# Local attention on block-diagonal keys and values, two heads at a time, in a fused attention and feed-forward kernel

## The chip, the cores and the metric

The kernel runs on one core of a Trainium2 chip. Times are device microseconds (us) of one execution. A run is called slow when it lies over 1.5% above the fastest of the same kernel; slow runs are left out of every ratio. The core has five engines that matter here: TensorE (PE in the profile; PEld is its weight load), VectorE (DVE), ScalarE (ACT), GpSimd (POOL) and SyncE (SP, which here only issues transfers). PEclk is the TensorE clock that was granted, as a share of full speed.

## The reference

```python
def _attn_ref(q, k, v):                      # each 8 batches x 8 heads x 576 x 64
    q_d, k_d, v_d = means of four rows       # 144 x 64
    out_d = sm_attn(q_d, k_d, v_d)           # full attention on the means
    out_up = np.repeat(out_d, 4, axis=2)
    mask = np.abs(pos[:, None] - pos[None, :]) < 4
    scores = np.where(mask, scale * q @ k.T, -1e9)
    out_local = softmax(scores) @ v          # a band of 7 keys
    return out_up + out_local

x = attention output, 4608 tokens x 512
out = gelu(x @ w_in) @ w_out                 # 512 -> 2048 -> 512, exact Gelu
```

So each batch has a small dense attention on 144 means, a banded one on 576 rows, and their sum feeds a feed-forward layer that carries most of the matrix work.

## The kernel before

The tokens are cut into nine chunks of 512. While TensorE does chunk c, the attention of batch c + 1 is woven into the gaps: its transposes into the first product (`m1`), its scores and values into the second (`m2`). `f1` and `f2` are fills: each call issues so many matmuls of the product.

```python
for c in range(NCH):
    b = c + 1
    f1 = filler(m1(c)) if c else f1_0
    ...
    elif b < B:
        v_down(b)                      # sums of four rows of v, five GpSimd instructions
        for p in range(NP):            # four pairs of heads
            f1(6 if p == 0 else 7)
            t_in(b, p, "q")
            f1(7)
            t_in(b, p, "k")
        k_lo()
    f1()
    f2 = filler(m2(c))
    ...
            attn(b, f2, 6, 9, 9)
    f2()
```

The local scores are five windows of 128 keys for each head, against a copy of k that is zero in the other head's rows. The values come out with the query on the partitions and a 65th column that sums the exponentials. VectorE divides by it, TensorE transposes the result back, and VectorE adds the two attentions into `xT`, the operand of the next first product.

```python
def norm(p, ps, half=None):
    ...
        nc.vector.reciprocal(out=rr, in_=av4[:, :, :, 64])
        nc.vector.tensor_tensor(out=nall..., in0=av4[:, :, :, 0:64], in1=rr..., op=ALU.mult)

def t_out(b, p):
    tr = ppool.tile([128, 1024], F16, tag="tr", name="tr_o")          # in PSUM
    ...                                                               # seven transposes
    nc.scalar.copy(out=xd, in_=tr[:, 576:720])
    nc.vector.tensor_tensor(out=xT[:, p, ...], in0=tr[:, 0:S]...,     # one operand in PSUM,
                            in1=xd.unsqueeze(2).broadcast_to(...), op=ALU.add)   # one in SBUF
```

The values of the next batch are loaded by GpSimd after each chunk. The output copies out of PSUM are on ScalarE. TensorE's two product banks alternate.

The softmax here doesn't subtract the row's maximum and nothing guards it: scores larger than these inputs give would overflow.

## Time and profile before

| | before |
|---|---|
| median of 3 runs | 353.62 us (352.41 to 353.96) |
| profiled span, granted clock | 348.4 us, 1.000 |
| TensorE busy | 97% |
| VectorE, ScalarE, GpSimd busy | 53, 55, 52% |
| one batch in the steady part | 20.33 + 15.89 = 36.22 us |

The prediction shows the lines behind this table. Two more stretches matter for what follows. The VectorE timeline of the first batch (start, us, engine, line, operation, output and input, count):

```profile
15.65 0.41 DVE L539 COPY q_nat<-q_nat 72x1024 f16<-72x1024 f16 x1
...
16.65 0.54 DVE L305 COPY KL<-kdz 64x64 f16<-64x64 f16 x2
```

These two copies go from SBUF to SBUF, and TensorE needs their results soon. They are short. The second stretch is a chunk boundary, from the timelines of GpSimd and VectorE:

```profile
143.29 1.27 POOL L312 TENSOR_TENSOR v_d<-v_t 128x512 f16<-128x512 f32 x1
...
144.17 0.76 DVE L445 TENSOR_TENSOR xT<-tr_o,xd 128x576 f16<-128x576 f16 x1 [2.11 <-ACT xd L444]
```

The add into `xT` takes 0.76 us while GpSimd is at its sums of v. Remember that its first operand, `tr_o`, lies in PSUM.

### The profile page before, as it was taken

What the parts mean: (1) busy time and instruction counts of PE and PEld (TensorE: products, weight loads), DVE (VectorE), ACT (ScalarE), POOL (GpSimd) and SP (SyncE); (2) the same over time, 40 slices, a digit from 0 to 9 for tenths busy, and PEclk for the clock granted to TensorE, in tenths of its full rate; (3) what the DMA queues carried; (4) which work ended last, traced back from release to release, by engine and by line L of the source; (5) the groups of instructions that cost most, each with busy time, mean ns of one, the idle gap of its engine ahead of it and who ended that gap; (6) DMA issues with size and microseconds to landing.
All of it is one profiled execution on the core that took longest, in us unless ns stands there. A gap on an engine that the chain in (4) does not pass through costs nothing.

```text
span 348.4 us, 7162 instructions
## 1 busy us (share of the span) xinstructions
PE 339.0 (97%) x2976; PEld 193.9 (56%) x2976; DVE 184.5 (53%) x338; ACT 192.8 (55%) x360; POOL 180.4 (52%) x243
## 2 busy tenths in 40 slices
PE   8898998999999999999999999999999999999996
PEld 4773455655665566555655575556655664444444
DVE  7793645747574857386747665676558470000000
ACT  3664465645764577357746764566556755614620
POOL 8957649633977298628963797369652000000000
PEclk9999999999999999999999999999999999999999
DMA  6999999920999099908990599129940001011002
GB/s 87 165 205 144 185 164 110 182 75 0 98 159 146 2 77 152 176 0 59 154 171 23 36 148 178 41 18 150 159 79 0 32 33 59 2 60 60 0 34 89
DMA packets 126543, 32.31 MB, mean 93 GB/s; under 512 B 109616, under 2 KB 122032, under 8 KB 126512
## 3 DMA queue, kind: packets, MB, share of 16 engines
q0 software_dynamic: 121184, 22.43, 82.2%
q1 hardware_dynamic: 5328, 9.44, 7.6%
q8 instruction: 23, 0.38, 0.4%
q14 instruction: 8, 0.07, 0.1%
HBM read 44.83 MB, written 9.44 MB: 156 GB/s over the span
## 4 chain that ended last, share of the span: by engine, by line
PE 88%; DMA 6%; DVE 2%; POOL 2%; issue 1%; ACT 0%; POOLq 0%
PE m_ps L224 35%; PE m_ps L200 33%; PE sc L348 4%; DMA w_in_sb<-in_moe_w_in_dram 3%; PE av L403 2%; PE tr_o L441 2%; DMA q_nat<-in_q_dram 2%; PE tr_k L237 2%; PE tr_q L237 2%; DMA k_nat<-in_k_dram 1%; DVE kz L272 1%; PE av L397 1%; PE sc L353 1%; PE m_ps L215 1%; PE av L395 1%; DVE kdz L275 1%
## 5 line engine op out<-in xcount | busy, mean ns | idle before, releaser
L200 PE MATMUL m_ps<-xT,w_in_sb 128*128 128x512 f16 x568 | 133.3, 379 | 0.5 <-ACT gT L195 0.5
L224 PE MATMUL m_ps<-w_out_sb,gT 128*128 128x512 f16 x560 | 130.3, 379 | 0.0
L203 ACT ACTIVATE gT<-m_ps 128x512 f16<-128x512 f32 x142 | 84.8, 597 | 56.7 <-PE m_ps L200 56.7
L200 PEld LDWEIGHTS <-w_in_sb 128*128 128x128 f16 x568 | 52.1, 97 | 54.7 <-issue 0.8
L224 PEld LDWEIGHTS <-gT 128*128 128x128 f16 x560 | 51.9, 98 | 54.6
L228 ACT COPY out_sb<-m_ps 128x512 f32<-128x512 f32 x35 | 20.6, 589 | 42.8 <-PE m_ps L224 37.8
L243 POOL TENSOR_TENSOR q_t<-qT 128x288 f32<-128x288 f16 x24 | 16.0, 667 | 52.0 <-DVE qT L240 37.8
L104 POOL DMA_DIRECT2D q_nat<-in_q_dram x42 | 32.6, 789 | 8.1 <-DMA w_out_sb<-in_moe_w_out_dram 5.7
L252 DVE TENSOR_REDUCE kdz<-kz 64x144 f16<-64x576 f16 x48 | 35.9, 747 | 1.5
L445 DVE TENSOR_TENSOR xT<-tr_o,xd 128x576 f16<-128x576 f16 x28 | 21.2, 758 | 26.9 <-ACT xd L444 26.9
L104 POOL DMA_DIRECT2D k_nat<-in_k_dram x42 | 32.2, 778 | 6.3 <-DMA w_in_sb<-in_moe_w_in_dram 3.5
L418 DVE TENSOR_TENSOR nall<-av,rr 128x896 f16<-128x896 f32 x29 | 31.7, 1091 | 1.0
L248 DVE COPY kz<-tr_k 64x576 f16<-64x576 f16 x48 | 21.9, 455 | 18.2 <-PE tr_k L237 17.5
L381 DVE TENSOR_TENSOR e<-e,band 128x1152 f16<-128x1152 f16 x28 | 21.0, 751 | 17.6 <-ACT e L375 17.6
L219 DVE COPY out_sa<-m_ps 128x256 f32<-128x256 f32 x2 | 0.8, 424 | 54.9 <-PE m_ps L215 54.9
L116 POOL DMA_DIRECT2D v_win<-in_v_dram x30 | 26.6, 912 | 0.0
L348 PE MATMUL sc<-qT,kz 128*128 128x112 f16 (+1 forms) x320 | 25.6, 214 | 0.0
L373 ACT ACTIVATE e<-sc 128x680 f16<-128x680 f32 x32 | 23.4, 732 | 2.0 <-PE sc L348 2.0
L348 PEld LDWEIGHTS <-kz 128*128 128x128 f16 x320 | 21.6, 97 | 0.9
L311 POOL TENSOR_TENSOR v_t<-v_grp 128x1024 f32<-128x1024 f16 x6 | 12.7, 2118 | 17.0 <-DMA v_grp<-in_v_dram 17.0
L444 ACT COPY xd<-tr_o 128x144 f16<-128x144 f16 x28 | 7.7, 276 | 22.0 <-PE tr_o L441 22.0
L375 ACT ACTIVATE e<-sc 128x472 f16<-128x472 f32 x32 | 18.2, 569 | 0.0
(168 smaller groups left out, 407.6 us busy)
## 6 DMA issues: line engine op xcount, KB each, us to landing
out_dram<-out_sb SPq DMA_DIRECT2D x35, 256.0 KB, 3.2
v_win<-in_v_dram POOLq DMA_DIRECT2D x40, 128.0 KB, 9.6
q_nat<-in_q_dram POOLq DMA_DIRECT2D x42, 96.0 KB, 3.7
k_nat<-in_k_dram POOLq DMA_DIRECT2D x42, 96.0 KB, 4.2
v_grp<-in_v_dram POOLq DMA_DIRECT2D x6, 512.0 KB, 8.8
w_in_sb<-in_moe_w_in_dram POOLq DMA_DIRECT2D x4, 512.0 KB, 8.1
w_out_sb<-in_moe_w_out_dram POOLq DMA_DIRECT2D x4, 512.0 KB, 9.4
v_lo<-in_v_dram POOLq DMA_DIRECT2D x6, 64.0 KB, 8.8
```

Of the source, the lines that this page charges most:

```text
L104: nc.gpsimd.dma_start(out=nat6(ld[b % 2][nm])[:, c, :, :], in_=src[b, :, CH * c:CH * c + CH, :].rearrange("h s d -> s h d"))
L116: nc.gpsimd.dma_start(out=L["vw"][:, j, :, 0:64], in_=v[b, :, W0[j]:W0[j] + 128, :].rearrange("h s d -> s h d"))
L200: nc.tensor.matmul(out=ps, lhsT=w_in_sb[:, fc, 128 * j:128 * j + 128], rhs=xT[:, fc, 512 * c:512 * c + 512], start=(fc == 0), stop=(fc == 3))
L203: nc.scalar.activation(out=g[:, j, :], in_=ps, func=ACTF.Gelu)
L224: nc.tensor.matmul(out=ps, lhsT=g[:, j, 128 * t:128 * t + 128], rhs=w_out_sb[:, j, :], start=(j == 0), stop=(j == NJ - 1))
L248: nc.vector.tensor_copy(out=kz[r, p, hh, :], in_=tr[r, 0:S])
L252: nc.vector.tensor_reduce(out=kdz[r, p, hh, :], in_=kz[r, p, hh, :].rearrange("p (g r) -> p g r", r=4), axis=AX.X, op=ALU.add)
L348: nc.tensor.matmul(out=dst, lhsT=kz[:, p, hh, W0[j]:W0[j] + 128], rhs=qT[:, p, Q0[j]:Q0[j] + QW[j]], start=(b > 0), stop=True)
L373: nc.scalar.activation(out=e2[:, :, 0:340], in_=sc2[:, :, 0:340], func=ACTF.Exp, scale=0.125)
L381: nc.vector.tensor_tensor(out=e2, in0=e2, in1=band.unsqueeze(1).broadcast_to([128, 2, S]), op=ALU.mult)
L418: nc.vector.tensor_tensor(out=nall.rearrange("p j a c -> p a j c"), in0=av4[:, :, :, 0:64], in1=rr.unsqueeze(3).broadcast_to([128, 2, 7, 6 ...
L445: nc.vector.tensor_tensor(out=xT[:, p, S * b:S * b + S].rearrange("p (g r) -> p g r", r=4), in0=tr[:, 0:S].rearrange("p (g r) -> p g r", r=4),
```

## The change

The intent is to take matrix work out of TensorE's stream in batches 1 to 7. Ten blocks of 64 keys hold two heads at once: k and v are kept block diagonal (128 x 128, zero off the blocks), so one matmul serves two heads. The values are the stationary operand and the exponentials move, so the result already has the layout of `xT` and the output transposes go. The denominators come from a matmul with ones, and 1/x is taken as Exp(-Ln x) on ScalarE. VectorE takes the output copies. Values are converted to 16 bit in DRAM by GpSimd and loaded from there by SyncE. The zeroes of the blocks are written once, by GpSimd, near the start. The core of the diff:

```diff
+    for i in range(2):
+        nc.gpsimd.memset(ld[i]["vw"].rearrange("p j a d -> p (j a d)").bitcast(F32), 0.0)
+    nc.gpsimd.memset(kb.rearrange("p a j c -> p (a j c)").bitcast(F32), 0.0)
 ...
-                    nc.scalar.copy(out=osb, in_=ps)
+                    (nc.scalar.copy if c >= NCH - 2 else nc.vector.tensor_copy)(out=osb, in_=ps)
 ...
+        for j in range(NW):                      # scores: ten blocks, two heads each
+            c = 512 * (j // 5) + QN[j] - SH * (j // 5)
+            nc.tensor.matmul(out=sc[:, c:c + QL[j]], lhsT=kb[:, p, j, :], rhs=qT[:, p, QN[j]:QN[j] + QL[j]],
+                             start=True, stop=True)
 ...
+        for g in range(2):                       # denominators
+            nc.tensor.matmul(out=sc[:, 512 * g:512 * g + SH], lhsT=ON2, rhs=e[:, SH * g:SH * g + SH], ...)
 ...
+        for j in range(NW):                      # values
+            nc.tensor.matmul(out=nm[:, c:c + QL[j]], lhsT=L["vw"][:, j, p, :], rhs=e[:, QN[j]:QN[j] + QL[j]], ...)
 ...
+    def norm_out(b, p):
+        nc.scalar.activation(out=lr[:, 0:S]..., in_=sc2[:, :, 0:SH], func=ACTF.Ln)
+        ...                                      # two more Ln
+        nc.scalar.activation(out=lr, in_=lr, func=ACTF.Exp, scale=-1.0)
+        nc.vector.tensor_tensor(out=xl..., in0=nm2[:, :, 0:SH], in1=lr[:, 0:S]..., op=ALU.mult)
+        ...                                      # up, in two halves
+                nc.vector.tensor_tensor(out=xT[:, p, y:y + z - a]..., in0=xl[:, a:z]...,   # both in SBUF
+                                        in1=up[:, a // 4:z // 4].unsqueeze(2).broadcast_to(...), op=ALU.add)
 ...
-        if b + 1 < B:
-            run(load_qk(b + 1))
-            run(load_v(b + 1))
+            if b + 1 < B:
+                v_cast(b + 1)
+                run(load_qk(b + 1))
+            attn(b, f2, 6, 9, 9)
```

`attn` also issues its fills differently: the last pair has four fills before its values and nine after them.

## The prediction

> **What bounds the kernel now.** I read the page's totals, then the chain, then a table of stretches, then the timeline of one batch. The totals and the chain (shares of the span):
>
> ```profile
> PE 339.0 (97%) x2976; PEld 193.9 (56%) x2976; DVE 184.5 (53%) x338; ACT 192.8 (55%) x360; POOL 180.4 (52%) x243
> PE 88%; DMA 6%; DVE 2%; POOL 2%; issue 1%; ACT 0%; POOLq 0%
> ```
>
> TensorE is busy 97% of 348.4 us and carries 88% of the chain; no other engine passes 55%. "Busy" can hide waits, so I cut the span at the start of the first and the second product of a chunk. The table of stretches for one steady batch (length in us, then each engine's busy us and instruction count, clock, DMA share, GB/s):
>
> ```profile
> 124.57:144.90 20.33, 20.33 (x217) 12.76 (x216) 12.36 (x19) 12.34 (x25) 17.61 (x21) 1.00 1.74 151
> 144.90:160.79 15.89, 15.89 (x113) 8.29 (x112) 10.89 (x21) 9.55 (x16) 7.00 (x13) 1.00 0.12 30
> ```
>
> The first is "second product of chunk b-1 with the attention of batch b in its gaps", the second "first product with the transposes of the next batch". Later batches repeat them to 0.02 us: a period of 36.22 us. Inside the first, the TensorE timeline (start, us, line, operands):
>
> ```profile
> 125.70 0.23 PE L353 MATMUL sc<-qd,kdz 128*128 128x144 f16 x1
> 126.35 2.10 PE L224 MATMUL m_ps<-w_out_sb,gT 128*128 128x512 f16 x9
> 128.29 0.41 PE L328 MATMUL sl<-qd,KL 128*128 128x144 f16 x4
> 128.54 0.23 PE L353 MATMUL sc<-qd,kdz 128*128 128x144 f16 x1
> 129.19 0.19 PE L395 MATMUL av<-v_d,ed 128*128 128x65 f16 x1
> 129.43 0.47 PE L403 MATMUL av<-v_win,e 128*128 128x65 f16 x10
> 129.74 2.10 PE L224 MATMUL m_ps<-w_out_sb,gT 128*128 128x512 f16 x9
> 131.68 0.22 PE L438 MATMUL tr_o<-I,nall 128*128 128x128 f16 x1
> 132.05 0.23 PE L353 MATMUL sc<-qd,kdz 128*128 128x144 f16 x1
> ```
>
> The distance of starts is the cost. Nine fills take 1.94 us (216 ns each), scores of a head pair 126.35 - 125.70 = 0.65, the low-key scores 0.25, the value product 129.74 - 129.19 = 0.55, the output transposes 132.05 - 131.68 = 0.37. Check: 64 x 0.216 + 4 x (0.65 + 0.55 + 0.37) + 0.25 = 20.35 against 20.33 shown. So TensorE waits for nothing here: what is taken from its stream is gained, and any new wait is lost.
>
> The work of the others in that phase, from the groups of instructions by shape:
>
> ```profile
> L203 ACT ACTIVATE gT<-m_ps 128x512 f16<-128x512 f32 x142 | 84.8, 597 | 56.7 <-PE m_ps L200 56.7
> L373 ACT ACTIVATE e<-sc 128x680 f16<-128x680 f32 x32 | 23.4, 732 | 2.0 <-PE sc L348 2.0
> L371 ACT ACTIVATE ed<-sc 128x288 f16<-128x288 f32 x32 | 13.0, 407 | 7.4 <-PE sc L348 7.3
> L418 DVE TENSOR_TENSOR nall<-av,rr 128x896 f16<-128x896 f32 x29 | 31.7, 1091 | 1.0
> L413 DVE TENSOR_TENSOR nall<-m_ps,rr 128x448 f16<-128x448 f32 x4 | 2.5, 624 | 0.1
> L381 DVE TENSOR_TENSOR e<-e,band 128x1152 f16<-128x1152 f16 x28 | 21.0, 751 | 17.6 <-ACT e L375 17.6
> L445 DVE TENSOR_TENSOR xT<-tr_o,xd 128x576 f16<-128x576 f16 x28 | 21.2, 758 | 26.9 <-ACT xd L444 26.9
> ```
>
> **Cost rules from them.** ScalarE: (732 - 407) / (680 - 288) = 0.83 ns an element on some 168 ns; in the timeline the next independent one starts 0.10 to 0.11 us before the previous ends. VectorE with a 32-bit operand: (1091 - 624) / 448 = 1.04 ns an element on 157 ns; the 16-bit mask runs at half of that per element (1152 in 751 ns), the broadcast add at the full price (576 in 758).
>
> **What the Trainium skill says.** "TensorE: Matmul & The Clock Gate", section Back-to-back issue gap, gives N / 2.4 + 2.5 ns per warm matmul and a floor near 25 ns; the trace agrees (512 columns 216 ns; the 65-column ones start 30 ns apart). "ScalarE: Activation LUTs", section What ACT_TABLE_LOAD costs, gives about 1283 ns for a load, and section Table sets says that one set holds both exp and ln; the trace has 1283 ns for each load, and cannot show the joint set. "VectorE: DVE Perf Modes", section What auto-detection actually checks, asks 16-bit operands of unit step for the doubled rate; the three VectorE rates above agree.
>
> **The change part by part, TensorE.** I price each matmul by the gap rule.
> - Scores of a pair: two of 144 columns (63 ns) and ten 53 to 61 wide (27 ns) instead of two and ten of 112 to 124: 0.126 + 0.265 = 0.39, so -0.26 us.
> - Output transposes go: -0.37.
> - Values: the 18 matmuls of 65 columns (0.55) become two for the column sums (288 columns, 122 ns: 0.245), four of 144 (0.25) and ten narrow (0.265): 0.76, so +0.21.
> Per pair -0.42, per batch -1.68, for seven batches -11.8 us, if nothing waits. Transposes on the way in stay.
>
> **ScalarE and VectorE.** Per pair ScalarE now does exp 288 (0.41), exp 576 (168 + 480: 0.65), Ln 576 (0.65), two Ln 144 (0.29 each), Exp 720 (0.77): 3.06 us against 0.41 + 0.73 + 0.57 + 0.28 = 1.99. The output copies (0.59 x 4) move to VectorE. With the low-key exp and two table switches of about 1.5 each: 12.2 + 0.3 + 3.0 = 15.5 of a phase of 20.33 - 1.68 = 18.65: no new bound by volume. VectorE per pair: mask 0.45, local product 0.76, two of 144 (0.31 each), add 0.76: 2.6; with four output copies (157 + 512 x 1.04 = 0.69) 13.1 us per phase. It fits too.
>
> **The latency is what counts.** Let s be the start of the ones matmuls of a pair. Ln may start at s + 0.245 + 0.17 (drain, from 0.38 busy against 0.216 distance) + 0.04 = s + 0.455. Ln, Ln, Ln with overlaps 0.55 + 0.19 + 0.29, then the dependent Exp 0.04 + 0.77: 1.84. VectorE: 0.03 + 0.67 + 0.22 + 0.31: numerators free at s + 0.455 + 1.84 + 1.23 = s + 3.53; the add, 0.04 + 0.76, has xT ready at s + 4.33.
> Between pairs TensorE fills: values 0.76, nine fills 1.94, scores 0.39, three fills 0.65, ones 0.245, so it asks for the single numerator buffer at s + 3.99. Slack 0.46 us: no wait in the middle pairs.
> At the last pair: values 0.76, nine fills 1.94, then three matmuls of the next first product (0.65), and the fourth needs xT of this pair: s + 3.35, ready at s + 4.36. **Wait of 1.0 us.** The VectorE copy of the last output tile then runs until about s + 4.96, while the second group of the first product asks for that bank at s + 4.58: **another 0.4**. In chunk 6 the copies stay on ScalarE, so that part falls away. The kernel before had thirteen fills plus five between values and the next chunk, and lost nothing there. Cost: 6 x 1.4 + 1.0 = +9.4 us.
>
> **Batch 1.** The downsampling on TensorE goes (53.50 to 54.82: -1.3) with the waits that the page shows behind it (0.76 + 0.20: -0.96). Against it: GpSimd zeroes three tiles of 2560 words before the loads of batch 1. Its 128-column memset took 205 ns against 102 ns for one column, 0.83 ns a word: 3 x 2.2 = 6.7 us, from 17.2 to 23.9. Twelve loads of 0.78 then end at 33.2 instead of 32.05; most is hidden, since the ring was full before:
>
> ```profile
> 27.67 1.55 POOL L104 DMA_DIRECT2D k_nat<-in_k_dram  x2 [1.97 <-DMA w_in_sb<-in_moe_w_in_dram]
> 34.71 0.46 PE L261 MATMUL tg_k<-I,k_nat 96*128 96x96 f16 x2 [0.17 <-DMA k_nat<-in_k_dram]
> ```
>
> I take +0.8. Eighteen v loads instead of five (some 0.7 each, 12 us), then 5.2 us of sums on GpSimd, end near 55, when the first value product asks: +0.5 for the risk. Sum for batch 1: -1.0.
>
> **Sum.** -11.8 + 9.4 - 1.0 = -3.4 us, on 353.6: 350.2. I choose 349.5, a little lower, because a chain worked out with every wait in series tends to come out long.
>
> **Rivals.**
> - The wait at the chunk boundary is hidden (Ln and Exp shorter, or the add at the doubled rate): -11.8 - 1.0 gives 341. For it: TensorE is the only bound. Against: the broadcast add took 758 ns with 16-bit operands.
> - VectorE becomes the bound in the first-product phase. It was busy 10.89 of 15.89; if the copies into 64-column blocks fall to the single rate (640 elements, about 0.82 instead of 0.5 us), each pair of heads needs 0.46 + 1.64 + 1.53 = 3.6 against TensorE's 3.54, the low-key block comes late, and about 1.2 us a batch are lost: 358. Against: runs of 64 elements were copied fast in the first batch (1024 elements in 478 ns).
> - The v path through DRAM comes late. The direct transfers took 8.8 to 9.6 us to land; the new ones wait in the SyncE queue with the outputs. For: sixteen more issues per batch, 332 ns each in the trace for an output. Against: the DMA share is 0.12 in the first-product phase, and values are needed some 25 us after the issue. It is hidden, I think; otherwise up to +2 us a batch, 360.
> - Table loads between Ln and Exp, if the joint set is not kept: eight more a batch, 10 us on ScalarE, above 400. The explicit preload speaks against it.
>
> **Range and chances.** The wait per boundary may lie between 0.3 and 2 us, that is 342.9 to 354.8 with the rest fixed; the ends being less likely, 344 to 354.5. Faster by over 2% needs below 346.5, a boundary wait under 0.8: 0.28. Slower by over 2% needs one of the last three rivals: 0.07.
>
> **What would show it.** Right: first-product stretches still about 15.9 us plus one TensorE wait of about a microsecond at each chunk's first group, released by VectorE's xT; second-product stretches about 18.7; the numerator tile never waited for; two table loads a batch. Wrong: TensorE waits in the middle pairs, released by the mask, the numerators or the sums; a wait for the low-key block at the phase start; v_win or v_grp as releaser; block copies near 0.8 us; or TensorE idle under 0.5 us per boundary.

## The result, and the profile after

| | before | after |
|---|---|---|
| median, same rounds | 353.01 us (351.28 to 353.96) | 376.93 us (373.37 to 382.04) |
| ratio of the fast runs | | 1.068 (95%: 1.060 to 1.075) |
| profiled span, granted clock | 348.4 us, 1.000 | 380.3 us, 0.954 |
| TensorE busy | 339.0 us | 344.0 us |

A ratio is the mean time of one kernel's fast runs over that of the other's of the same rounds, so it isn't quite the ratio of the medians. The predicted time was 349.5 us; the kernel got 6.8% slower.

The profile of after fell on the slowest of its four runs, 382.04 us, called slow. What I read in it shows in fast profiles of the experiments too, in like sizes: a held copy at the start of 6.93 us in e2 and of 8.02 in e8, adds at the boundaries of 1.95 to 3.33 us in e8. Totals and the chain that ended last:

```profile
PE 344.0 (90%) x2718; PEld 187.3 (49%) x2718; DVE 218.7 (57%) x413; ACT 209.3 (55%) x387; POOL 169.9 (45%) x228
...
PE 72%; POOL 9%; DMA 7%; DVE 5%; issue 4%; ACT 2%; SPq 0%; POOLq 0%; DVEq 0%
```

TensorE has 258 matmuls less and is busy 5 us more, and its share of the chain fell from 88 to 72%. So it waits now, and part of its work runs at half clock. One batch in the table of stretches (length in us, then busy us and count of TensorE, its weight load, VectorE, ScalarE and GpSimd, the granted clock, DMA share and GB/s):

```profile
102.80:121.83 19.03, 19.03 (x181) 10.99 (x180) 11.53 (x27) 14.18 (x29) 8.72 (x12) 1.00 1.40 159
121.83:143.22 21.39, 17.86 (x114) 8.82 (x112) 15.60 (x25) 10.14 (x17) 10.81 (x15) 0.92 0.23 50
```

The first line, second product with attention, is 19.03 us against 20.33 before, without a wait: the gain is there. The second, first product with transposes, is 21.39 against 15.89, with TensorE busy for only 17.86 of it and the clock at 0.92: the loss is there. Who is waited for, from the view of waits (us in total, times, longest):

```profile
PE m_ps L229 <- DVE xT L423: 14.2, 7, 2.7
PE m_ps L606 <- DVE q_nat L598: 8.6, 2, 7.8
PE m_ps L229 <- DVE out_sb L257: 4.6, 5, 1.9
```

In both of the large ones TensorE waits for VectorE. The timelines of one boundary, GpSimd, VectorE and TensorE:

```profile
162.95 2.11 POOL L336 TENSOR_TENSOR v_t<-v_grp 128x1024 f32<-128x1024 f16 x1 [10.05 <-DMA v_grp<-v]
...
163.27 2.41 DVE L423 TENSOR_TENSOR xT<-xl,up 128x576 f16<-128x576 f16 x1
...
165.73 0.38 PE L229 MATMUL m_ps<-xT,w_in_sb 128*128 128x512 f16 x1 [2.68 <-DVE xT L423]
166.45 0.59 PE L229 MATMUL m_ps<-xT,w_in_sb 128*128 128x512 f16 x2 [0.35 <-DVE out_sb L257]
...
167.14 2.83 PE L229 MATMUL m_ps<-xT,w_in_sb 128*128 128x512 f16 x7
```

The add into `xT` took 2.41 us and ended 0.6 us after GpSimd's first sum (which ends at 165.06). Seven matmuls that take 1.68 us at full clock then took 2.83. At the seventh boundary no batch is left, and GpSimd does nothing:

```profile
320.66 0.76 DVE L423 TENSOR_TENSOR xT<-xl,up 128x576 f16<-128x576 f16 x1
...
321.47 0.38 PE L229 MATMUL m_ps<-xT,w_in_sb 128*128 128x512 f16 x1 [1.03 <-DVE xT L423]
```

The same add is 0.76 us and the wait 1.03. And the start, VectorE, GpSimd and TensorE:

```profile
15.67 8.63 DVE L598 COPY q_nat<-q_nat 72x1024 f16<-72x1024 f16 x1
...
17.40 4.44 POOL L207 MEMSET v_win<- 128x2560 f32 x2
21.74 2.27 POOL L208 MEMSET kb<- 128x2560 f32 x1
...
24.35 0.66 PE L606 MATMUL m_ps<-I,q_nat 72*128 72x72 f16 x8 [7.85 <-DVE q_nat L598]
```

The copy that took 0.41 us took 8.63 us and ended at 24.30, 0.3 us after the last memset.

Where the 31.9 us between the two spans are: up to the second product of chunk 1 (it starts at 102.80 against 88.19) 14.6 us, of which 11.2 before the first product of chunk 0 (39.97 against 28.82); in the next five periods (37.9 to 40.6 us each, together 197.8 against 5 x 36.22 = 181.1) 16.7 us; after that 0.6.

**Theory** (L in the expectations). VectorE and GpSimd hold each other up at SBUF. The Trainium skill says so on "SBUF — State Buffer", section Who interferes with whom: the two share a second pair of ports, as an exclusive lock; a VectorE instruction with two SBUF inputs contends with a GpSimd instruction that reads SBUF, and a VectorE copy in a two-port mode with any, and the other "fully blocks". The add of before had one operand in PSUM; that of after has two in SBUF. **Rivals.** The boundary wait is only the longer chain Ln, Exp, product, add (C); the long copy at the start is a transfer's work (D), or an accident of the changed order; or the new transfers (SyncE's value loads) hold everything up.

### The profile page after: what moved, and what is told of

The parts are those of the page before. It is cut to its first block, busy times and chain, and to the rows that moved or that the text cites. A ratio compares the mean times of both kernels' runs of the same rounds, so it can differ in the third digit from the quotient of the medians.

```text
span 380.3 us, 7000 instructions
## 1 busy us (share of the span) xinstructions
PE 344.0 (90%) x2718; PEld 187.3 (49%) x2718; DVE 218.7 (57%) x413; ACT 209.3 (55%) x387; POOL 169.9 (45%) x228
## 4 chain that ended last, share of the span: by engine, by line
PE 72%; POOL 9%; DMA 7%; DVE 5%; issue 4%; ACT 2%; SPq 0%; POOLq 0%; DVEq 0%
PE m_ps L229 30%; PE m_ps L253 28%; DMA v_grp<-in_v_dram 4%; PE nm L400 2%; DMA q_nat<-in_q_dram 2%; PE sc L372 2%; PE tr_q L274 2%; PE sc L390 2%; PE tr_k L274 2%; POOL v_win L131 2%; DVE out_sb L257 1%; ACT lr L410 1%; POOL k_nat L121 1%; DVE xl L413 1%; PE nm L396 1%
## 5 line engine op out<-in xcount | busy, mean ns | idle before, releaser
L413 DVE TENSOR_TENSOR xl<-nm,lr 128x576 f16<-128x576 f32 x28 | 21.2, 758 | 28.2 <-ACT lr L410 28.2
L287 DVE TENSOR_REDUCE kdz<-tr_k 64x144 f16<-64x576 f16 x48 | 36.3, 755 | 0.7
L266 DVE COPY kb<-tr_k 64x640 f16<-64x640 f16 x48 | 23.5, 489 | 22.0 <-PE tr_k L274 21.7
L423 DVE TENSOR_TENSOR xT<-xl,up 128x576 f16<-128x576 f16 (+2 forms) x36 | 31.5, 894 | 1.0
L384 DVE TENSOR_TENSOR e<-e,band 128x576 f16<-128x576 f16 x28 | 15.1, 538 | 28.0 <-ACT e L379 28.0
L407 ACT ACTIVATE lr<-sc 128x576 f32<-128x576 f32 x28 | 18.2, 651 | 10.9 <-PE sc L390 10.9
L410 ACT ACTIVATE lr<-lr 128x720 f32<-128x720 f32 x28 | 22.5, 803 | 0.9
L257 DVE COPY out_sb<-m_ps 128x512 f32<-128x512 f32 x28 | 19.4, 691 | 0.8
L379 ACT ACTIVATE e<-sc 128x576 f16<-128x576 f32 x28 | 18.0, 644 | 0.0
L131 POOL DMA_DIRECT2D v_win<-in_v_dram x16 | 10.7, 699 | 10.7 <-DMA w_out_sb<-in_moe_w_out_dram 8.7
```

The costliest lines, as they stand in the source:

```text
L131: eng.dma_start(out=ld[b % 2]["vw"][64 * hh:64 * hh + 64, 5 * g:5 * g + 5, p, 64 * hh:64 * hh + 64], in_=bass.AP(x.tensor, x.offset, [[D, ...
L257: (nc.scalar.copy if c >= NCH - 2 else nc.vector.tensor_copy)(out=osb, in_=ps)
L266: nc.vector.tensor_copy(out=kb[r, p, :, 64 * hh:64 * hh + 64].rearrange("q (g i) c -> q g i c", g=2), in_=bass.AP(x.tensor, x.offset, [x.a ...
L287: nc.vector.tensor_reduce(out=kdz[r, p, hh, :], in_=tr[r, 0:S].rearrange("p (g r) -> p g r", r=4), axis=AX.X, op=ALU.add)
L407: nc.scalar.activation(out=lr[:, 0:S].rearrange("p (g c) -> p g c", g=2), in_=sc2[:, :, 0:SH], func=ACTF.Ln)
L410: nc.scalar.activation(out=lr, in_=lr, func=ACTF.Exp, scale=-1.0)
```

## The experiments

Twelve kernels, all correct. The first four share the runs of before with a median of 351.24 us, the next four of 351.51, then three of 351.58, the last of 351.17. Each is built on after, or on the run named.

**e1: the GpSimd memsets later in its order.**

```diff
-    for i in range(2):
-        nc.gpsimd.memset(ld[i]["vw"]...)
-    nc.gpsimd.memset(kb...)
 ...                                   # after half of batch 1's q and k loads:
+    nc.gpsimd.memset(kb...)
 ...                                   # after the second weights' loads:
+    for i in range(2):
+        nc.gpsimd.memset(ld[i]["vw"]...)
```

> Edit: the three GpSimd memsets go later in GpSimd's order: the block-key tile after the six q loads of batch 1, the two value tiles after the output weights. Theory L (VectorE operations that need a second SBUF port wait while GpSimd holds it): the last re-ordering copy of batch 0's queries, 8.63 us in the changed kernel, falls to about 0.45 us, TensorE's 7.8 us wait for it goes, and with it the half-clock matmuls that follow: total about 366 us (changed kernel 375.7 in fast runs). Rival D (the copy waited for its data, a q load delayed by the longer GpSimd order): the copy stays at several us and the time stays within 2 us of 375.7. Lock on a mask or copy elsewhere may shift a little of it to batch 1.

Measured: 374.4 us, ratio 1.062 (1.056 to 1.068). A miss. The q_nat copies were short again (0.58 us at most), but the lock found another copy (VectorE, then GpSimd):

```profile
33.41 7.13 DVE L674 COPY BH<-B 64x64 f16<-64x64 f16 x1
...
36.06 4.45 POOL L659 MEMSET v_win<- 128x2560 f32 x2
```

This set-up copy of 64 columns stood for 7.13 us, and TensorE waited 4.2 us for what VectorE does after it. So the memsets do it wherever a copy from SBUF to SBUF meets them; moving them is no cure. (The profiled run was slow; the copy was held in the same way in e4, 6.39 us, in a fast one.)

**e2: the sums of v after the first pair's transposes.**

```diff
         elif b < B:
-            v_down(b)
             for p in range(NP):
 ...
                 t_in(b, p, "k")
+                if p == 0:
+                    v_down(b)
```

> Edit: for batches 2 to 7 the value sums on GpSimd are issued after the first pair's transposes instead of at the start of the first product; nothing else. Theory L: the last add into xT of a batch, 1.76 to 3.15 us at the six boundaries where GpSimd sums beside it, falls to 0.76 us as at the seventh; TensorE's wait there falls from 2.0-2.7 (plus up to 1.9 for the output copy) to about 1.0 plus 0.35, and the half-clock stretch after it goes: about 2 us a boundary, total 362 to 366 us. Rival C (the wait is the length of the Ln/Exp chain, or values come late): the sums only move later, so the time stays at 375 or grows.

Measured: 362.12 us, ratio 1.030 (1.027 to 1.033), as expected. The add is 0.76 us everywhere (0.83 in two parts, in the two batches where the end of the ring of `xT` cuts it). Five of the seven boundaries wait the expected 1.03 + 0.35 us, those two 0.83 + 0.61 and 0.63 + 0.81. One boundary, VectorE, GpSimd and TensorE:

```profile
155.19 0.76 DVE L423 TENSOR_TENSOR xT<-xl,up 128x576 f16<-128x576 f16 x1
...
159.35 2.12 POOL L336 TENSOR_TENSOR v_t<-v_grp 128x1024 f32<-128x1024 f16 x1
...
156.00 0.38 PE L229 MATMUL m_ps<-xT,w_in_sb 128*128 128x512 f16 x1 [1.03 <-DVE xT L423]
156.73 0.59 PE L229 MATMUL m_ps<-xT,w_in_sb 128*128 128x512 f16 x2 [0.35 <-DVE out_sb L257]
```

From 1.068 to 1.030 are 13 us. The chain of Ln, Exp, product and add and the new transfers are as they were, so neither of these rivals made the longer wait. But the stretches of this fast run still don't beat the 36.22 us of before:

```profile
135.13:154.16 19.03, 19.03 (x181) 10.98 (x180) 11.28 (x24) 14.18 (x29) 8.66 (x12) 1.00 1.36 155
154.16:171.74 17.58, 16.20 (x113) 8.29 (x112) 13.45 (x24) 10.13 (x17) 10.42 (x15) 1.00 0.31 66
```

19.03 + 17.58 = 36.61. The boundary costs 17.58 - 15.88 = 1.70, more than the 1.38 of waits shown: in a stream a matmul of 0.379 us starts 0.216 after the one before, after a wait it can't overlap with it. So two waits lose 2 x 0.163 us, and 1.38 + 0.33 = 1.71.

**e3: the local values stay in PSUM, so that the add has one SBUF operand.** The sums stay where the change has them.

```diff
-        xl = wpool.tile([128, S], F16, tag="xl", bufs=2, name="xl")
-        nc.vector.tensor_tensor(out=xl..., in0=nm2[:, :, 0:SH], in1=lr..., op=ALU.mult)
+        nc.vector.tensor_tensor(out=nm2[:, :, 0:SH], in0=nm2[:, :, 0:SH], in1=lr..., op=ALU.mult)
 ...
-                    in0=xl[:, a:z]...
+                    in0=nm2[...]...
```

> Edit: the sums stay at the boundary; the local product is written back into PSUM and the add into xT reads it there, so it has one SBUF operand instead of two. Theory L: the add takes about 0.76 us at every boundary although GpSimd runs beside it, and the boundary wait falls to about 1.2 us as in the run with the sums moved; but the numerators' buffer is freed 0.8 us later, so middle pairs wait some 0.35 us each (21 of them, 7 us): total 366 to 373. Rival C: the add stays above 1.7 us where GpSimd runs, and the time does not fall.

Measured: 379.6 us, ratio 1.080. A miss in time. The disputed thing itself came out as the theory says (GpSimd, then VectorE):

```profile
159.78 2.12 POOL L336 TENSOR_TENSOR v_t<-v_grp 128x1024 f32<-128x1024 f16 x1 [11.01 <-DMA v_grp<-v]
161.97 1.27 POOL L339 TENSOR_TENSOR v_d<-v_t 128x512 f16<-128x512 f32 x1
...
161.85 0.76 DVE L420 TENSOR_TENSOR xT<-nm,up 128x576 f16<-128x576 f32 x1
```

The add beside GpSimd's sums is 0.76 us (and the second sum, v_d, 1.27 instead of the 1.66 it took beside the add at 163.27 of after: there it was held in turn), and no boundary waits over 1.2 us for it. The loss came from what I had priced too low: the numerators' only buffer now stays occupied until the add, and for that I had 0.35 us in each of 21 middle pairs, 7 us. TensorE did wait for it 21 times, but 0.59 to 0.93 us each, 7.1 + 5.0 + 3.6 = 15.7 us. The start kept its lock, too (TensorE waited 6.4 us).

**e4: e1 and e2 together.** The diffs are those above.

> Edit: the two moves together. Theory L: the gains add, about 10 and 12 us, to 352 to 356 us, that is within 1% of the kernel before; what remains above the predicted 349.5 is the late value load of batch 1 (TensorE waits 2 to 3 us for it in the changed kernel). If the total stays above 360, a cost is missing in the account.

Measured: 360.65 us, ratio 1.026. A miss, in part for e1's reason: the set-up copy took 6.39 us and another 3.29. By the expectation's own test (above 360) a cost was missing in the account: the period stayed at 36.6 us, as in e2.

**e5: e2, and no GpSimd memset before batch 1.** The key blocks and one value tile are zeroed by ScalarE at the very start (2.31 us each), the other value tile by GpSimd after batch 1's sums.

```diff
+    for t in (kb..., ld[1]["vw"]...):
+        nc.scalar.copy(out=t..., in_=zf)
-    (the three GpSimd memsets)
 ...
             v_down(1)
+            nc.gpsimd.memset(ld[0]["vw"]..., 0.0)
```

> Edit: sums moved as in e2_vdown; and no GpSimd memset at the start: ScalarE zeroes the block keys and the value tile of batch 1 in its idle time before the first scores, GpSimd zeroes the other value tile after the sums of batch 1. e1_memset showed that the lock only moved to later copies (7.13 us on a 64-element copy). Theory L: no VectorE copy above 1 us before batch 1, TensorE's 7 us wait at the start gone, first product of chunk 0 starts near 29 us as before the change; the collision with the sums of batch 1 (low-key copy and mask, some 3 us) stays. Total 354 to 357 us. Rival: the start is slow for another reason, and 360 stays.

Measured: 361.38 us, ratio 1.028. A miss in time, though no VectorE copy took over 0.8 us: the lock at the start is gone. The time is the rival's, but not for its reason: the first product of chunk 0 began at 29.26 us, as expected. The earlier start was lost to the next wait: TensorE stood 5.8 us for batch 1's grouped values (v_d) and 1.6 for v_lm. They are late because GpSimd issues batch 1's eighteen value loads itself ahead of its sums.

**e6: e5, with batch 1's values also through DRAM and SyncE.**

```diff
     run(load_qk(1))
+    v_cast(1)
 ...
-    vg_load(1, nc.gpsimd, v[1])
-    vw_load(1, nc.gpsimd, v[1])
+    vg_load(1, nc.sync, v16[1])
+    vw_load(1, nc.sync, v16[1])
```

> Edit: e5_start, and batch 1's values also go through the 16-bit copy in DRAM and the SyncE queue, so GpSimd issues one transfer instead of eighteen and its sums of batch 1 come earlier, in the first product. Theory: masks and low-key copy of batch 1 run at their own length, no TensorE wait for the values of batch 1: 2 to 4 us less than e5_start, 351 to 354. Rival: the extra copy delays the output weights, and TensorE waits for them at the first second product: no gain.

Measured: 357.38 us, ratio 1.018 (1.014 to 1.021). The gain on e5, 4.0 us, is at the upper end of the 2 to 4 expected; the time misses 351 to 354 because e5 had missed. The wait for v_d fell to 1.1 us, but the grouped values took 13.5 us to land beside the second weights, and GpSimd waited 17.6 us for them.

**e7: e6, with the fills around the attention moved, so that more of the second product follows the last pair.**

```diff
-            attn(b, f2, 6, 9, 9)
+            attn(b, f2, 6, 4, 8)
```

> Edit: e6_v1, and the fills are dealt out anew: 4 instead of 9 before the first mask, 8 instead of 9 after each pair, so that eight more (1.73 us) stand between the last pair of a batch and the next first product. Theory: the boundary wait of 1.03 + 0.35 us and its after-effects (1.7 us, seen in e2_vdown) go nearly to zero; the middle pairs have the slack of 0.4 us for one fill less: 9 to 11 us less than e6_v1, 341 to 345, faster than the kernel before by over 2%. Rival: the middle pairs start to wait for the numerators or the sums, half of the gain goes: 346 to 349.

Measured: 356.89 us, ratio 1.015 (1.009 to 1.021). A miss of both ranges. TensorE no longer waited for `xT` at all, but now 0.67 to 0.74 us at each of the seven boundaries for the product bank (4.8 us in all): the copies of the third and fourth output tile both stand behind the last normalisation in VectorE's order. The period was 36.13 us.

**e8: the same fills on after alone.**

> Edit: the changed kernel with nothing but the new dealing of fills (4 and 8). Theory: the add into xT still waits for GpSimd at the boundary, so it takes 1.7 to 3 us, but 1.73 us more of fills stand beside it: the boundary wait halves, with less half-clock after it; the start is untouched: 362 to 367. If the chain alone made the boundary wait (rival C), the wait would vanish here and the time fall to 360 or below.

Measured: 369.97 us, ratio 1.053 (1.047 to 1.058). It gained about 1.4%, less than expected; the waits moved to the output copies (13.0 us at seven boundaries, 3.2 at most), which stand behind the held add (1.95 to 3.33 us). Rival C, by which the wait goes and the time falls to 360 or below, did not come. At the start the KL copies took 8.02 us this time instead of q_nat's 8.63: which copy is caught is a matter of a microsecond.

**e9: e7, the third tile's copy ahead of the last normalisation and the fourth's on ScalarE.**

```diff
-                    (nc.scalar.copy if c >= NCH - 2 else nc.vector.tensor_copy)(out=osb, in_=ps)
+                    (nc.scalar.copy if c >= NCH - 2 or t == 3 else nc.vector.tensor_copy)(out=osb, in_=ps)
 ...
-                fill(4)
+                fill(5)
```

> The run before, with the last pair's fill raised from 4 to 5 and the output copy of each chunk's fourth tile on ScalarE. Theory: what is left at the boundary is the two output copies that VectorE can only make after the last normalisation, 0.67 us a boundary, 4.8 us in seven; with the third tile's copy ahead of the last normalisation and the fourth on the idle ScalarE the TensorE waits for output copies fall to 1 us in all, the period from 36.1 to 35.4-35.6 us, and the time from 356.9 to 352 (350 to 354). Rival: the wait only moves, to the last normalisation's xT or to the first Gelu behind ScalarE's copy; then the period stays at 36.0-36.3 and the time at 355-358.

Measured: 348.36 us, ratio 0.990 (0.986 to 0.994), 4 us better than the theory. (The profiled run was slow; the period is the same in the fast profiles of e10 and e12.) No boundary waits for `xT` or an output copy any more. The period is 131.64 - 96.55 = 35.09 us.

**e10: e9, with batch 1's grouped values loaded straight by GpSimd, before the second weights.**

```diff
-    v_cast(1)
+    vg_load(1, nc.gpsimd, v[1])
     for f in range(4):
+        if f == 2:
+            v_cast(1)
         nc.gpsimd.dma_start(out=w_out_sb[:, 4 * f:4 * f + 4, :], ...)
-    vg_load(1, nc.sync, v16[1])
```

> The same, and batch 1's grouped values loaded straight by GpSimd ahead of the second weights, its values' conversion in DRAM between the halves of those. Theory: batch 1 loses 4.3 us (2.6 + 1.7) only because its sums start at 53.7 us; with the load earlier they are done before the first value product, TensorE waits for v_d and v_lm under 0.5 us, and the time falls by about 4 against the run without it, to 348 (346.5 to 350.5), below the kernel before. Rival: the load takes the transfers that the second weights need (their wait grows from 0.4 to 2-3 us), or the early sums hold VectorE's set-up copies (a copy of over 2 us near 40); then 350.5 to 354.

Measured: 346.42 us, ratio 0.985 (0.982 to 0.989). The gain on e9 is 1.9 us where 4 were expected; the time is at the lower end of the range because e9 had come out low. The sums are done by 46.1 us and are not waited for, but the windows of v, behind the weights, are (3.6 us).

**e11: the kernel before, with nothing but three GpSimd memsets.**

```diff
     nc.vector.memset(KL.bitcast(F32), 0.0)
+    scr = w_out_sb.rearrange("p j c -> p (j c)")[:, 0:5120].bitcast(F32)
+    for i in range(3):
+        nc.gpsimd.memset(scr, 0.0)
```

> The kernel before with nothing changed but three GpSimd memsets of 128 x 2560 words, put where the change has them, into space that the second weights fill later. Theory (a running GpSimd memset keeps VectorE from SBUF-to-SBUF copies): the copy of q_nat near 15.7 us or of KL near 16.7 us, 0.4 and 0.27 us now, takes 6 to 8.6 us, TensorE waits 6 us or more for it, and the time rises by 6 to 9 us, to 357.5-360.5. Rival (the long copy needs the rest of the change, or comes of the transfers): no VectorE copy over 1 us, the time rises by at most 1.5 us, the delay of twelve loads behind the memsets: 351.5-353.

Measured: 355.51 us, ratio 1.012 (1.007 to 1.016). The long copy is there (VectorE, GpSimd, TensorE):

```profile
15.28 0.41 DVE L542 COPY q_nat<-q_nat 72x1024 f16<-72x1024 f16 x1
...
16.28 5.76 DVE L308 COPY KL<-kdz 64x64 f16<-64x64 f16 x2
...
17.44 6.85 POOL L182 MEMSET w_out_sb<- 128x2560 f32 x3
...
22.43 0.24 PE L356 MATMUL sc<-qd,kdz 128*128 128x144 f16 x1 [4.04 <-DVE qd L566]
```

Two copies of 64 columns, 0.54 us before, take 5.76 (3.47 the longer one), and nothing else of the change is in this kernel. That settles that the memsets alone hold VectorE. The first product of chunk 0 began 6.0 us later (34.80 against 28.82), its second product 4.6 (53.94 against 49.36), and the time rose by 4: under the expected 6 to 9, perhaps since VectorE got in between the second memset and the third, and chunk 0 has other waits that took up part of it; I didn't separate these.

**e12: e10, the conversion of batch 1's values ahead of all the second weights.**

```diff
+    v_cast(1)
     for f in range(4):
-        if f == 2:
-            v_cast(1)
```

> The run before, with batch 1's conversion of the values ahead of all four second-weight loads instead of between them. Theory: the 3.6 us that TensorE waits for v_win in batch 1 is only the conversion's place in the queue; started some 1.5 us earlier and with 1.1 MB less ahead of it, it lands about 5 us earlier, the wait for v_win is under 0.5 us, that for the second weights grows from 1.3 to about 2.5, and the time is 344.5 (343 to 345.7). Rival: the transfers of this stretch (busy at 0.9 or more of the time) only change places: the second weights are waited for by 3 us or more, or v_win still is, and the time stays at 345.7-348.

Measured: 344.65 us (341.96 to 346.0), ratio 0.980 (0.975 to 0.984): faster than before by about 2%, but the interval reaches to both sides of the 2% line, so whether it is over 2% is unclear. The time is as expected, the wait only in part: 2.0 us for the windows remained, and 1.5 for the second weights. One batch of this run, in the view of stretches:

```profile
89.31:108.51 19.20, 19.18 (x181) 10.91 (x180) 12.93 (x30) 15.37 (x30) 8.65 (x12) 1.00 1.43 163
108.51:124.39 15.88, 15.88 (x113) 8.29 (x112) 11.37 (x21) 9.54 (x16) 10.41 (x15) 1.00 0.28 62
```

TensorE has hardly a gap in either stretch (0.02 us in the first). With 35.08 us a batch the mended change gains 1.14 on the 36.22 of before, once no boundary waits.

## Why the prediction was wrong

**TensorE's stream: right, the size a little off.** Predicted -1.68 us a batch. The undisturbed stretch is 19.03 us in after and in e2, that is -1.30. In e2's timeline the scores of a pair take 0.42 us instead of the 0.39 worked out, ones and values 0.79 instead of 0.76 (0.94 in the last pair): pricing each matmul by the gap rule came out a little low. With e9's fills the stretch is 19.20 us: in e12's timeline the values of a pair start 0.25, 0.43, 0.30 and 0.35 us after the ones, so with eight fills between the pairs the numerators' buffer is asked for just before it is free.

**Volume of ScalarE and VectorE: right.** From batch 2 on no middle pair waited in after; in batch 1 TensorE waited 0.18 us for the mask and 0.72 for the numerators' buffer. The block copies took 489 ns, not the 820 of the rival; there were two table loads of 1283 ns a batch; the dependent Exp of 720 columns took 803 ns for 770 predicted.

**The boundary wait: this is the step that failed.** "The add, 0.04 + 0.76, has xT ready at s + 4.33", and from it "wait of 1.0 us" and "another 0.4". Where GpSimd is idle the waits shown agree to 0.05 us: 1.03 + 0.35 at the seventh boundary, and at five of seven in e2. That is luck in part. At the seventh boundary the ones start at 316.75 and `xT` is ready at 321.42, s + 4.67 and not s + 4.36, mainly since the three Ln don't overlap as priced (they start at 317.19, 317.88 and 318.18); and TensorE asks at s + 3.53, not s + 3.35, so the two errors nearly cancel. The second wait is there although the prediction has it fall away in chunk 6: it misread `c >= NCH - 2`, which leaves the copies on ScalarE in chunks 7 and 8 alone. At the other six boundaries the add took 1.76 to 3.15 us (both parts together where it is cut) instead of 0.76, because both its operands now lie in SBUF and GpSimd reads there at the same time. The 758 ns came from a row of before in which one operand was in PSUM (`xT<-tr_o,xd`): I took over the duration and overlooked what made it safe. e3 shows the condition (0.76 us with one operand in PSUM, beside the same sums), e2 the effect (13 us). To the longer add comes the clock: after the waits the next matmuls ran for 3.41 us at half of it, 2.2 to 2.8 us for seven instead of 1.68 at five of the six.

**What a wait costs.** Even unlocked, a boundary of 1.03 + 0.35 us of waits cost 1.70, because the sum left out the overlap lost after each wait. So e2 had -1.30 + 1.70 = +0.4 a batch where the sum had -1.68 + 1.4 = -0.3. The change as laid out had no steady gain to give, lock or no lock.

**Batch 1 and the start: mis-sized.** "Most is hidden", with +0.8 for the memsets. I had priced them as time on GpSimd only. The first product of chunk 0 began 11.2 us later in after, behind a held copy of VectorE. With nothing but the memsets moved it began at 29.62 (e1; 29.83 in e4, a fast run) instead of 39.97, so 10.3 of these us hang on the memsets' place; in e11 the memsets alone delayed it by 6.0 and the end by 4. For batch 1's values I took +0.5; once the start was mended they cost 5.8 + 1.6 us (e5), and a whole series of runs (e6, e10, e12) went into bringing that to some 3.5, with the wait for the second weights.

**The rivals.** None of the four happened. The nearest was the late v path: its transfers did not come late for the value matmuls, but their landing at the boundary put GpSimd's sums beside the add. The hidden boundary wait, 341 us, is what e9 to e12 had to build: with it before is beaten, by 6.5 us in the medians of e12.

**What stays open.** The 10.3 us that hang on the memsets at after's start are not all the lock; I did not separate the half clock after the hold and the later loads in them. The gain from e7 to e9 is 8.5 us in the medians where 4.8 of waits were seen. The period fell by 36.13 - 35.09 = 1.04 us, which in seven batches makes 7.3: 0.67 of it is the wait and 0.16 the overlap lost after it. The other 0.2 a batch, and the last 1.2 us, I did not trace; the six runs of e9 alone lie 5.6 us apart.

## What to carry to other kernels

When a VectorE instruction's operand moves from PSUM to SBUF, its duration alone no longer tells its cost: look at what GpSimd does at that moment. Keep GpSimd's big memsets and sums away from copies from SBUF to SBUF and from two-operand VectorE work that TensorE waits for, or give the zeroing to an engine that is idle. Where TensorE is 97% busy, a saving in its stream is only worth what is left after the new waits, so move work across the boundary first (copies ahead of the last normalisation, more fills behind it).

## What the Trainium skill lacked or had wrong

- "SBUF — State Buffer", section Who interferes with whom: its rule for two-input instructions holds here (0.76 us alone or with one operand in PSUM, 1.76 to 3.15 us beside GpSimd's sums), and so does that for copies (0.41 us became 8.63 beside memsets). A copy can also stand before the memset's recorded start, of which the section says nothing: it stood from 15.67 with memsets from 17.40 (after), from 16.28 with 17.44 (e11) and from 33.41 with 36.06 (e1). In between GpSimd was only issuing transfers, beside which the q_nat copy takes 0.41 us in before. GpSimd's spans are rough in this profile, so the memset's recorded start may be late; that stays open.
- The same section speaks of one instruction against one. In a row of three memsets of 2.3 us VectorE got in between them in e11 (two copies held 5.76 us in all, ending at 22.04 while the third memset ran to 24.29), but only after all three in after (8.63 us) and for a pair of copies in e8 (8.02 us). No page says which.
- "TensorE: Matmul & The Clock Gate", section What's actually happening, has the clock fall after an idle window of about 3.4 us. No wait at a boundary here was that long, and yet a single one of 2.04 us was followed at once by three matmuls in 1.73 us (0.81 at full clock); a wait of 2.31 + 0.35 us at another boundary left the clock alone, as did 1.03 + 0.35. The half-clock stretches after after's boundaries are 3.41 us long and their starts (85.59, 126.55, 167.51, 205.06, 246.02) lie whole multiples of that apart. Cut on this grid, TensorE was idle for 60% of the piece before 205.06, and the 2.31 + 0.35 us fell on two pieces, 30 and 48% idle. So a piece need not be idle throughout.
